# Queries of five pairs transposed from the landed fp32, masks drawn in slot order, and a new order of work

## The chip, the cores and the metric

The kernel runs on one core of a Trainium2 chip. The metric is the device time of one execution in microseconds; lower is better. The engines are named as the profile names them: PE is TensorE's matmul stream and PEld its weight loads, DVE is VectorE, ACT is ScalarE, POOL is GpSimd, SP is the engine that issues nearly all transfers. Each engine takes its instructions in the order in which they were recorded.

## The reference

Attention over 4 batches, 8 heads, 768 positions and a head size of 64, followed by a gated feed-forward block on the 3072 tokens of 512 features.

```python
causal = rel >= 0
is_sink = pos[None, :] < int(n_sink)                 # n_sink = 4
in_win = (rel >= 0) & (rel < int(window))            # window = 64
stream_keep = causal & (is_sink | in_win)
# heads 0, 2, 6 use causal; the other five use stream_keep
a = softmax(where(mask, scale * q @ k.T, -1e9)) ; x = a @ v
g = x @ w_gate                                       # 512 x 1536
out = (g * sigmoid(g) * (x @ w_val)) @ w_out         # 1536 x 512
```

Inputs and output are fp32; inside, the kernel multiplies in fp16 and accumulates in fp32.

## The kernel before, in words

**Tiles.** A pair is 256 positions of one batch; there are 12, and `QP` lists them, the pairs of the first two batches interleaved. A pair has two tiles of 128 positions, so there are 24 tiles. The 24 tiles go in six groups of four to the feed-forward part. Positions are held in slot order: a pair's load puts position 2p + j at partition p, and after the transposes the even positions of a tile come first, then the odd ones.

**A pair's way in.** `load` brings q, k and v of a pair (512 KB each) into a buffer of the ring `raw` (14 buffers). `cast` turns k and q into fp16 in a buffer of the ring `hq`. For pairs 0 to 4 (`XQK = XK = 5`) TensorE then transposes: `transposes(n, w)` does eight 128x128 blocks for q (w = 0, line 438) or k (w = 1, line 435) into PSUM, and `evacq` and `evack` copy them to `qT` and `kT`. From pair 5 on the transfers transpose instead (`dmaq`, `dmak`), from the buffers `hqz` and `hq`. `hqz` is cleared once by `fill3`.

**A tile.** `scores` (line 547) multiplies keys and queries into PSUM, `exps` (line 557, ACT) takes the exponential, `values` (line 577) multiplies by v, `recip` and `norm` divide, `xtranspose` turns the result for the feed-forward part. A tile's scores come in two to four units; units of tiles 0 and 1 are up to 512 elements wide and may sit in the ring `gv`, those of later tiles up to 1024 wide and always sit in the one buffer of the ring `sc`, which is two PSUM banks.

**Masks.** GpSimd draws four 128x128 patterns (`OWN`, `DIAG`, `FAR`, `BAND0`) into `nat` in natural order, 0 where a key is kept and -32768 where not. For tiles 0 to 3 the scores get them added on TensorE: a matmul of `nat` by the permutation matrix `perm` into the same PSUM bank (`marks`). For later tiles the exponentials are multiplied by 0/1 masks `m0`, `m1`, `m2` (line 565). `mask_order` (line 245) multiplies `perm` and `nat` once into PSUM, and `mask_fill` (line 255, DVE) writes the 0/1 masks from there in nine operations.

**Feed-forward.** `gate` (line 778) multiplies a group's tiles by one 128-column block of the gate or the value weights; `tanh` (784, ACT), `stt1` (788, DVE) and `stt2` (795, DVE) form h; `outproj` (813) multiplies by the output weights, `oevac` copies out of PSUM, `store` writes. The weights are cast by `wcast` from fp32 loads of 512 KB.

**What sets the order.** All work is recorded as tasks (`P.add`), each with the engines that may run it. The strings `ORDER` and `WAYS`, worked out beforehand, give the sequence in which the tasks are recorded and the engine each one takes; nothing is rescheduled afterwards. A number of 3700 + n in `ORDER` stands for n more `warm` matmuls (line 292), fillers of 512 columns whose result nobody reads. Waits follow from what a task reads and from the ring buffer that it takes. The task names used below are: `cq`/`ck`/`cx` n.x, casts of q, k, v of pair n; `trn.0` and `trn.1`, transposes of q and k; `evqn.sx` and `evkn.x`, their evacuations; `sct.u`, `ext.u`, scores and exponentials of unit u of tile t; `valt.o`, `nmt.o`, values and norm; `xtrt`, the transpose of tile t; `gateg.j.c`, gate of group g, block j; `wc g1`, the cast of the second gate weight load; `mkdiag`, `mkfar`, the mask drawing; `mfill`, the mask fills.

Read out of `ORDER` and `WAYS`, the order before is, up to the first gate:

```
PE   warm(10) tr0.0 warm(2) tr0.1 warm(6) sc1.3 tr1.0 sc1.2 sc1.0 sc0.1 sc0.0 tr1.1 val0.0 val0.1
     sc1.1 sc2.0 val1.0 tr2.0 val1.1 sc3.0 warm(1) val2.1 xtr0 sc3.1 val3.1 xtr1 warm(1) val2.0
     tr2.1 gate0.2.0
ACT  cq0.0 cq0.1 evq0.00 evq0.10 evq0.11 evk0.0 ex1.3 ex1.2 ex1.0 evq1.00 ex0.1 ex0.0 ex1.1 ex2.0
     nm0.0 ex3.0 cx1.1.0 xe1 ex3.1
DVE  fill ck0.0 evq0.01 evk0.1 fill3 cx0.1.0 evq1.01 cx0.1.1 ck1.0 evq1.10 evq1.11 evk1.1 evk1.0
POOL mkdiag ck0.1 mkfar cq1.0 cq1.1 cx0.0.0 ck1.1 fill1 cx0.0.1 cq2 cx1.0.0 cx1.0.1 ck2
SP   q0 k0 q1 v0 k1 q2 v1 k2 g1 g0 wv1 q3 wv0 k3 g2
```

On SP `g` and `wv` are loads of gate and value weights. Behind the first gate, `xtr2` and `sc4.0` follow within the next seven tasks of PE.

Of the kernel before, what the change touches and what calls it, by code (L numbers as in the profile page):

```python
# [7 lines left out]
FP = mybir.dt.float32  # L8
FH = mybir.dt.float16
AF = mybir.ActivationFunctionType  # L10
ALU = mybir.AluOpType
# [5 lines left out]
    "080400091L1O021M1N01xh1T1U1W1V1Xxi1Y1a1Z1K0B0A1Rxm1t1u25261P0C280E031Q2D1r2G1S1s271n1d1o1b2E2j2I"  # L17
    "2F1e2H1i1c1f2K1p0D1q292A2J2L1g0F1y2p2k1h1j2M2C2r2q1v0j1w1k151x2V2Wxh2N1z202O2P0i0p1l2B1m2X2Z2a23"
    "242b2Yxh2Q2s9Z2R2S2c2t2T2d210H2U9j11309k312e9l109F0o2h2u9G162i9o9a9H9c2v0I0k0G9b9d3Q059e062x9f9p"
    "9q9m3W2y369n3D3Y9K0q9g22072z129I3E3X9J2f9N9L9M3A3B3M3R3Z3a9O189h2l2m9t9u9i2w3e9v9y0K329P333f9z9r"  # L20
    "9s34A00n350t3b2n37199w9x2o3C0m3cA13F3G1H3H3IA249134FAN3J4G9QAO9R3h9S9T3i3K1IAQ3g3pAP1E3z0s401FAS"
    "4HAR3d9UAV0J3S3TATAUAW3N9V3t380l3L3VAI0L9W3u1BAL3vAJ393j3k3l3mAKA8AM4A410N3n9X3o0r0O9Y3q4I423wA9"
    "3xA34o0M3U434J44ADAA4N3r4p3y3sAG453OAEAF0Q2g1CA44O4K4WABAH4q463P4L4BA54748A64Z4aBQ4MACA70xBTBR4c"
    "4l4dAwAx4vBS4CBU4xBf4PBg4DAyBh4Q4RBVBWAzBXB0ArAsB14bAtBiBj4S4w4TB24y5253B3B44U4VBGBH4z50B5BJBL5V"
    "0RBI4f0w5WBY4X4E4hBK5X1AB64gB75D4e5G5H0v17BZ1D510yB80u14BkAX5J4iB9BA0zBl4Y4j1J5K5fAY0PBM1GBNBm55"
    "4m564r54BaBEAZAa4k5L5d4s594t4u575A5cAu585B5E5eBb5g5hAvAc0T5CAdBc0bAe5I5Q5MBO0SBP5Z0UBB5N5O5RAfBC"
    "BDAhBd5P0VAi5S5TAjAb5oBFAk5pBnBeAg625Y634n64Bo5FAmAn5iAo5UCJ6761ApCd7SCKCL5r5s5tCeCf6BCgCh6ACsBp"
    "Bq5q5a68COCtCu5j7T5k695yAq656F5bCv5u7Q0X6i5v6GCPCQAlBr0W6g6CBs0a6O6p5w5x6DCwC95lCACB6ECMBuCR6UCS"
    "BvCNBwCn6V6I6hCoCpCb0Z6J6oBx6qBt0Y5zCY6kCZCaCcCT6X665m6Y6nBzCi6K6R6S7P0e6HC0C1Cl6LCjCkCmCCCUCV6M"
    "6d7W6uCD0g6T5n6v6NCE6P6w7XC260CHCxCFCGCI6rC46s7N6mC5Cy6z706Z6aCW6jCXCz6W6b6xCqC36QD08a6y7x6c6fCr"  # L30
    "6eC6C7By7O7VD2757U6tD37RD1787971D5D47AEF72E0E1E20c73D67B7C0hD7EDD876EGC87j7kEHEIEJEAEBECD9DA7D7g"
    "7t8i7l0d7vDRDB82DgDC7hEE7i7E7477DhDiE37m7n7z7FE5DSDTE6DDDEDF837GE47wE8Db7H6l7uE7E98eDUDVDcEK7I7Y"
    "7JENELEM7qEO7Z7aDHDIDd7KDe7LDq80817o0fDrDs7p877rDfDJ7yDKDWDXDYDt7b7cDu88DlDm847sDo8GDnDp857d8ZDv"
    "Dw8A7e8BDx89Dy8Y7MDM8JDG8KDjDzDk8LDN8MDZ7fEoEp8NFDFEDa868V8CFG8D8P8Q8c8E8gEqEjFFDOFH8dDPEkFIElDL"
    "EmFJ8f8h8pFL8FFKFMF88H8REP8qF9FA8jEn8k8bEQ8SEyEzFBERFC8m8lESETFS8xF0Et8nF18OEu8T8U9394F2EvEUEV8I"
    "ErEw8W8t8X90FTFUFcEW8oEx918r8uFdFe92FfEXDQ8sFX8v8wFg8y98EZFYEYEaFZ9996EsF3F495F58zEbEc979AF6FN9B"
    "9C9DEeEfF7FOFPFaFbFVEgFW9EGGEhGJEiGHGIGKGkGlGuGvGnGwGmFhFQGoGxGyFRG6G7FiFjFkFlEdG8GVGWGYGXGaG9Gb"
    "GcGZFmGpFnGqGrG1G2GAG3GsGBGtGCGdGeGDFoGLGMFpG4G5GQFrGRGSFsGTFtGOFuGNGfGgFvGPFqFwGhGEGFFxFyFzG0GU"
    "GiGzGjH0H1H4H2H3H5H6H7H8H9HAHBHEHFHCHDHGHHHJHIHKHL"
)  # L40
WAYS = (
    "000000000000000000000000000000000000000000000000000000000000002020222122002102002000012221100010"
    "001000000000100000000000000000101221222020011101100000000000000000000110022100001101001000000000"
    "100000100000000000002222220000100000100000000010000100100000000002022220110100000100000020000000"
    "100000010012202210000001001000000000100000010000000002221202000000000000000001000010022211210000"
    "000000000000220000001000000110202022000000000000000000000000000000000000012122000000000000000000"
    "010000210002221100000000010000001200010010000002001120011000000000000000000210000000000000000000"
    "000000000000000000000000000000000000000000000000000000000000000000000000000000000000000000000001"
    "000000000000000000000000000000000000000000000000000000000000000000000100001000000000000000000000"
    "000000000000000000000000000000000000000000000000000000000000000100000000000000000000000000000000"  # L50
    "000000000000000000000000000000000000010000100001000000000000000000000000000000000000000000000000"
    "000000000000000000000100000000000000000000000000000000000000000000000000000000000000000000000000"
    "10000000001000000010"
# [52 lines left out]
def kernel(  # L106
# [97 lines left out]
    perm = const.tile([128, 128], FH, name="perm")  # L204
# [7 lines left out]
    OWN, DIAG, FAR, BAND0 = range(4)  # L212
# [4 lines left out]

    def keep(n, base, qstep, kstep):
        nc.gpsimd.affine_select(
            out=nat[:, n], in_=nat[:, n], compare_op=ALU.is_ge, fill=OFF, base=base,  # L220
            pattern=[[qstep, 2], [2 * qstep, 64]], channel_multiplier=kstep)

    def make_diag():
        nc.gpsimd.memset(perm, 0.0)
        nc.gpsimd.affine_select(
            out=perm, in_=perm, compare_op=ALU.not_equal, fill=1.0, base=0,
            pattern=[[-1, 2], [-2, 64]], channel_multiplier=1)
        nc.gpsimd.memset(nat, 0.0)
        keep(DIAG, 0, 1, -1)
        keep(BAND0, WIN - 1, -1, 1)  # L230
        nc.gpsimd.memset(nat[0:NSINK, BAND0], 0.0)
        keep(BAND0, 0, 1, -1)

    def make_far():
        keep(OWN, WIN - 1, -1, 1)
        keep(OWN, 0, 1, -1)
        keep(FAR, WIN - 1 - 128, -1, 1)
        nc.gpsimd.memset(nat[0:64, FAR], OFF)
        nc.gpsimd.memset(nat[0:NSINK, FAR], 0.0)

    mask_ps = []

    def mask_order():
        ps = buf("o", [128, 4, 128], FP, "mk")
        nc.tensor.matmul(ps.rearrange("p n q -> p (n q)"), perm,
                         nat.rearrange("p n q -> p (n q)"), start=True, stop=True)
        mask_ps.append(ps)

    def mask_fill(x):
        ps = mask_ps[0]  # L250
        for dst, src in ((m2[:, 0:1], OWN), (m2[:, 1:4], DIAG), (m2[:, 4:5], FAR),
                         (m1[:, 0:2], OWN), (m1[:, 2:4], FAR),
                         (m0[:, 0:4], BAND0), (m0[:, 4:6], DIAG), (m0[:, 6:7], BAND0),
                         (m0[:, 7:8], DIAG))[5 * x:5 + 5 * x]:
            nc.vector.tensor_scalar(
                out=dst, in0=ps[:, src].unsqueeze(1).to_broadcast([128, dst.shape[1], 128]),
                scalar1=-1.0 / OFF, op0=ALU.mult, scalar2=1.0, op1=ALU.add)

# [32 lines left out]

    T_masks = [P.add("mkdiag", ["POOL"], make_diag)]
# [5 lines left out]
    T_mord = P.add("mord", ["PE"], mask_order, deps=T_masks, takes=["o"], after=[T_warm])  # L301
    T_fill = [P.add(f"mfill{x}", ["DVE"], (lambda x=x: mask_fill(x)), deps=[T_mord])
              for x in range(2)]
    P.uses(T_mord, "o", *T_fill)
# [72 lines left out]
    def cast(n, kd, x):  # L377

        r = landed[kd, n].rearrange("p (h j d) -> p h j d", j=2, d=64)
        if n >= XQK and kd == "q":  # L380
            recast(T_c[n, kd, x],
                 hqz[:, :, x, :, x * 64:(x + 1) * 64].rearrange(
                     "p j (r k) d -> p k r j d", r=2),
                 r.rearrange("p (k s r) j d -> p s k r j d", r=2, s=2)[:, x])
            return
        if n not in hqs:
            h = buf("hq", [128, 2, 1024], FH, "hq")
            hqs[n] = [h[:, 0].rearrange("p (j r x) -> p j r x", j=2, r=2),
                      h[:, 1].rearrange("p (k a x) -> p k a x", k=2, a=4)]
        if kd == "k":  # L390
            ks = slice(0, 2) if x is None else slice(x, x + 1)
            recast(T_c[n, kd, x],
                 hqs[n][1][:, ks].rearrange("p k a (s d) -> p k s a d", s=2),
                 r.rearrange("p (k s r) j d -> p k s (r j) d", r=2, s=2)[:, ks])
            return
        js = slice(0, 2) if x is None else slice(x, x + 1)
        recast(T_c[n, kd, x],
             hqs[n][0].rearrange("p j r (k d) -> p k r j d", d=64)[:, :, :, js],
             r[:, :, js].rearrange("p (k r) j d -> p k r j d", r=2))
# [28 lines left out]
    def transposes(n, w):  # L428
# [504 lines left out]
```

The softmax here doesn't subtract the row's maximum and nothing guards it: scores larger than these inputs give would overflow.

## Time and profile before

| | |
|---|---|
| median of 3 runs | 257.31 us (257.26 to 257.41) |
| the profiled execution | 257.29 us, span 255.5 us |
| first score matmul | 9.23 us |
| first gate matmul | 21.38 us |
| last matmul group ends near | 251.7 us |
| transfers in all | 42.53 MB |

The span is what the profiler recorded of the program; the execution's own time has 1.8 us around it. Times within a trace count from the start of the span. A timeline row gives the start, the duration, the engine, the source line, the operation, what it writes and reads, and in brackets how long the engine sat idle before it and what released it. A group row gives the number of instructions, the busy time and the mean duration of one. Durations of matmuls include a latency that overlaps with the next one, so a run of matmuls is counted by its start and end and not by the sum of its rows.

### The profile page before, as it was taken

Reading aid. Unit: us, or ns where it says so; the run is one execution under the profiler, and the core shown is the slowest. Engines: PE = TensorE matmul, PEld = TensorE weight load, DVE = VectorE, ACT = ScalarE, POOL = GpSimd, SP = SyncE. Lnnn points to the kernel's source line nnn. Section 1 sums busy time; section 2 is a strip of 40 time slices with the busy share of each in tenths; the row PEclk is TensorE's granted clock in tenths of the full one; section 3 lists DMA queues with packets and bytes.
Section 4 is the critical chain, followed back from the end, with each engine's and each line's share of the span. In section 5 each row is a group of like instructions: output and inputs, shape, how many; then the busy total and the mean of one; then the engine's idle time right before and its main releaser. Section 6 shows DMA issues by size and latency. Waiting matters only on the chain.

```text
span 255.5 us, 4847 instructions
## 1 busy us (share of the span) xinstructions
PE 246.7 (97%) x1812; PEld 136.7 (54%) x1812; DVE 177.1 (69%) x360; ACT 135.3 (53%) x214; POOL 81.5 (32%) x118
## 2 busy tenths in 40 slices
PE   7889899999999999999999999999999999999994
PEld 3567765665555554545555555555555554444442
DVE  3777899997897566859976587778557766463511
ACT  3767998766488445645555663637753412322100
POOL 4674888695674412410450230342000100000000
PEclk9999999999999999999999999999999999999999
DMA  7999999996999958998959947254022211300444
GB/s 188 290 310 326 318 337 316 304 212 136 388 181 223 295 140 158 266 167 189 224 114 204 239 91 165 44 116 92 0 62 64 62 23 41 82 0 0 100 96 99
DMA packets 80536, 42.53 MB, mean 166 GB/s; under 512 B 32768, under 2 KB 76032, under 8 KB 80512
## 3 DMA queue, kind: packets, MB, share of 16 engines
q1 hardware_dynamic: 80352, 42.09, 68.8%
q8 instruction: 14, 0.23, 0.4%
q10 hardware_dynamic: 160, 0.13, 0.2%
q14 instruction: 10, 0.08, 0.1%
HBM read 28.31 MB, written 6.29 MB: 135 GB/s over the span
## 4 chain that ended last, share of the span: by engine, by line
PE 84%; DVE 6%; DMA 3%; ACT 3%; SPq 2%; issue 1%; POOL 1%; DVEq 0%; POOLq 0%; ACTq 0%
PE gv L778 44%; PE o_ps L813 24%; PE sc L547 9%; PE av L577 5%; DMA raw<-in_k_dram 3%; ACT e L557 2%; SPq L317 2%; DVE h L795 1%; DVE sil L788 1%; DVE xb L594 1%; DVE vt L181 1%; DVE e L565 1%; ACT qT L175 1%; DVE qT L177 1%; PE xtr L610 1%
## 5 line engine op out<-in xcount | busy, mean ns | idle before, releaser
L557 ACT ACTIVATE e<-sc 128x1024 f16<-128x1024 f32 (+3 forms) x71 | 62.2, 878 | 32.1 <-PE sc L547 31.3
L778 PE MATMUL gv<-xt,wv_sb 128*128 128x512 f16 (+1 forms) x304 | 73.5, 368 | 0.4 <-DVE sil L788 0.3
L778 PE MATMUL gv<-xt,wg_sb 128*128 128x512 f16 (+1 forms) x304 | 73.0, 368 | 0.0
L784 ACT ACTIVATE sig<-gv 128x512 f32<-128x512 f32 (+1 forms) x76 | 43.0, 574 | 51.1 <-PE gv L778 49.4
L813 PE MATMUL o_ps<-wo_sb,h 128*128 128x512 f16 (+2 forms) x300 | 69.5, 370 | 0.0
L788 DVE SCALAR_TENSOR_TENSOR sil<-sig,gv 128x512 f32<-128x512 f32 (+1 forms) x76 | 49.3, 654 | 25.1 <-ACT sig L784 24.0
L795 DVE SCALAR_TENSOR_TENSOR h<-sil,gv 128x512 f16<-128x512 f32 (+1 forms) x76 | 49.3, 654 | 20.3 <-PE gv L778 18.9
L813 PEld LDWEIGHTS <-h 128*128 128x128 f16 x300 | 28.5, 98 | 30.0
L778 PEld LDWEIGHTS <-wg_sb 128*128 128x128 f16 x304 | 28.8, 98 | 27.2 <-issue 0.2
L778 PEld LDWEIGHTS <-wv_sb 128*128 128x128 f16 x304 | 28.7, 98 | 25.9 <-issue 0.6
L547 PE MATMUL sc<-qT,kT 128*128 128x256 f16 (+1 forms) x276 | 37.4, 257 | 0.5 <-ACT e L557 0.5
L565 POOL TENSOR_TENSOR e<-e,m 128x640 f16<-128x640 f16 (+1 forms) x16 | 26.3, 1641 | 33.9 <-ACT e L557 32.2
L547 PEld LDWEIGHTS <-kT 128*128 128x128 f16 x276 | 24.6, 98 | 12.3 <-issue 1.3
L577 PEld LDWEIGHTS <-e 128*128 128x128 f16 x472 | 19.6, 97 | 11.1 <-DVE xb L594 2.2
L577 PE MATMUL av<-vt,e 128*128 128x65 f16 x472 | 22.0, 193 | 1.3 <-DVE xb L594 0.5
L175 ACT COPY o_sb<-o_ps 128x512 f32<-128x512 f32 (+1 forms) x14 | 8.1, 578 | 26.0 <-PE o_ps L813 26.0
L594 DVE TENSOR_TENSOR xb<-av,rc 128x256 f16<-128x256 f32 x47 | 19.9, 424 | 1.6
L177 POOL CAST vt<-raw 64x512 f16<-64x512 f32 x24 | 15.5, 644 | 16.0 <-DMA raw<-in_v_dram 14.9
L177 POOL CAST hq<-raw 128x1024 f16<-128x1024 f32 (+1 forms) x15 | 14.2, 947 | 15.7 <-DMA raw<-in_k_dram 14.4
L177 POOL COPY vt<-vt 2x330 f16<-2x330 f16 x14 | 6.3, 453 | 37.6 <-PE av L577 37.3
L582 DVE RECIPROCAL rc<-av 128x4 f32<-128x4 f32 x48 | 8.5, 177 | 10.4 <-PE av L577 10.1
L565 DVE TENSOR_TENSOR e<-e,m 128x1024 f16<-128x1024 f16 (+1 forms) x22 | 14.7, 668 | 0.8 <-ACT e L557 0.8
(58 smaller groups left out, 130.9 us busy)
## 6 DMA issues: line engine op xcount, KB each, us to landing
raw<-in_q_dram SPq DMA_DIRECT2D x12, 512.0 KB, 6.5
raw<-in_k_dram SPq DMA_DIRECT2D x12, 512.0 KB, 7.0
raw<-in_v_dram SPq DMA_DIRECT2D x12, 512.0 KB, 7.0
out_dram<-o_sb SPq DMA_DIRECT2D x46, 128.0 KB, 2.4
raw<-in_moe_w_gate_dram SPq DMA_DIRECT2D x6, 512.0 KB, 7.8
raw<-in_moe_w_val_dram SPq DMA_DIRECT2D x6, 512.0 KB, 7.9
raw<-in_moe_w_out_dram SPq DMA_DIRECT2D x6, 512.0 KB, 6.7
xt<-xb SPq DMA_TRANSPOSE x16, 2.4
```

The costliest lines, as they stand in the source:

```text
L175: nc.scalar.copy(out=dst, in_=src)
L177: ENG[task.way].tensor_copy(out=dst, in_=src)
L547: nc.tensor.matmul(sc[c // 4][:, c % 4:c % 4 + n, :], weights, moving, start=first, stop=last)
L557: nc.scalar.activation(out=e[:, 0:n], in_=whole_sc.pop((t, u))[:, 0:n], func=AF.Exp, scale=scale)
L565: ENG[task().way].tensor_tensor(out=ev, in0=ev, in1=mm, op=ALU.mult)
L577: nc.tensor.matmul(av[:, n, 0:65], ee, vv, start=(m == 0), stop=(m == len(bl) - 1))
L594: nc.vector.tensor_tensor(out=xbs[t][:, :, odd, :], in0=av[:, :, 0:64], in1=rc.to_broadcast([128, 4, 64]), op=ALU.mult)
L778: nc.tensor.matmul(ps, wsb[:, kk, j * 128:(j + 1) * 128], xt[:, kk, c[0]:c[1]], start=(kk == 0), stop=(kk == 3))
L784: nc.scalar.activation(out=sg[g, j, c], in_=gs[g, j, c], func=AF.Tanh, scale=0.5)
L788: nc.vector.scalar_tensor_tensor(out=sl[g, j, c], in0=sg.pop((g, j, c)), scalar=1.0, op0=ALU.add, in1=gs.pop((g, j, c)), op1=ALU.mult)
L795: nc.vector.scalar_tensor_tensor(out=hs[g, j][:, c[0]:c[1]], in0=sl.pop((g, j, c)), scalar=0.5, op0=ALU.mult, in1=vs.pop((g, j, c)), op1=A ...
L813: nc.tensor.matmul(o_open[g, tt, x], hs[g, j][:, tt * 128:(tt + 1) * 128], wo_sb[:, j, lo:hi], start=(j == 0), stop=(j == NJ - 1))
```

## The change

Four things are changed together.

**Queries of pairs 0 to 4** are no longer cast. TensorE transposes them from the landed fp32 buffer with an fp32 identity, in two tasks of four blocks, one for each half s, each into a PSUM bank of its own (`ring_q`: the ring `tr` for s = 0; `gv` for s = 1 of pairs 0 and 1, `o` for later ones). Four evacuations for each pair, 64x512, fp32 to fp16. Before, pairs 0 and 1 had four of 64x512 and pairs 2 to 4 two of 64x1024, all from fp16. The `hq` buffer halves.

**Masks** are drawn by GpSimd in slot order, each pattern in two halves of 64 partitions, so scores add them through `ident` and `perm` is gone; `identf`, the fp32 identity, is drawn in its place. `mask_order` is gone. `mask_fill` reads `nat` from SBUF instead of PSUM and may run on ACT or DVE.

**The order** is a new one. `fill3` goes from DVE to POOL, `mfill0` and `mfill1` stay on DVE and come early. Read out of the new strings, up to the first gate:

```
PE   warm(10) tr0.0.0 tr0.0.1 warm(8) tr0.1 warm(5) tr1.1 sc1.3 sc1.1 sc1.2 sc0.0 tr1.0.0 warm(3)
     val0.1 tr1.0.1 sc1.0 tr2.0.1 sc0.1 sc2.0 val1.1 tr2.1 sc3.1 val0.0 val1.0 tr2.0.0 val2.1 sc3.0
     xtr0 val2.0 xtr1 sc4.0 xtr2 val3.1 gate0.2.0
ACT  ck0.0 ck1.0 evk0.1 evk0.0 ex1.3 cx0.0.0 ex1.1 evk1.1 ex0.0 evq1.01 evq1.00 ex1.2 ex1.0 ex2.0
     ex0.1 ex3.1 evq2.00 evq2.01 ex3.0 sk1.1 xe1 ex4.0
DVE  fill evq0.00 evq0.01 mfill0 evq0.10 ck1.1 evq0.11 evk1.0 mfill1 evq1.11 evq1.10
POOL mkident mkdiag mkfar fill3 ck0.1 cx0.1.0 fill1 cx0.1.1 cx0.0.1 cx1.0.0 cx1.0.1 wc_v1 cx1.1.1
     sk0.1 wc_g1
SP   q0 k0 k1 v0 q1 q2 k2 v1 wv1 g1 g0 v2 q3 wv0 k3
```

For pairs 3 and 4 the evacuations of q were two on ACT (pair 3) and two on DVE (pair 4); they are now three on ACT and one on DVE (pair 3) and one on ACT and three on DVE (pair 4).

The diff, cut to its core (the two strings are left out):

```diff
-    perm = const.tile([128, 128], FH, name="perm")
+    identf = const.tile([128, 128], FP, name="identf")
...
-    OWN, DIAG, FAR, BAND0 = range(4)
+    DIAG, BAND0, OWN, FAR = range(4)
...
+    def odds(j):
+        return slice(64 * j, 64 * j + 64)
+
     def keep(n, base, qstep, kstep):
+        for j in range(2):
+            part = nat[odds(j), n]
+            nc.gpsimd.affine_select(
+                out=part, in_=part, compare_op=ALU.is_ge, fill=OFF, base=base + kstep * j,
+                pattern=[[0, n.stop - n.start], [qstep, 2], [2 * qstep, 64]],
+                channel_multiplier=2 * kstep)
+
+    def first_keys(n, count, value):
+        for j in range(2):
+            nc.gpsimd.memset(nat[64 * j:64 * j + count // 2, n], value)
+
+    def make_identf():
+        nc.gpsimd.memset(identf, 0.0)
         nc.gpsimd.affine_select(
-            out=nat[:, n], in_=nat[:, n], compare_op=ALU.is_ge, fill=OFF, base=base,
-            pattern=[[qstep, 2], [2 * qstep, 64]], channel_multiplier=kstep)
+            out=identf, in_=identf, compare_op=ALU.not_equal, fill=1.0,
+            base=0, pattern=[[-1, 128]], channel_multiplier=1)
 
     def make_diag():
-        nc.gpsimd.memset(perm, 0.0)
-        nc.gpsimd.affine_select(
-            out=perm, in_=perm, compare_op=ALU.not_equal, fill=1.0, base=0,
-            pattern=[[-1, 2], [-2, 64]], channel_multiplier=1)
-        nc.gpsimd.memset(nat, 0.0)
-        keep(DIAG, 0, 1, -1)
-        keep(BAND0, WIN - 1, -1, 1)
-        nc.gpsimd.memset(nat[0:NSINK, BAND0], 0.0)
-        keep(BAND0, 0, 1, -1)
+        nc.gpsimd.memset(nat[:, DIAG:OWN + 1], 0.0)
+        keep(slice(BAND0, OWN + 1), WIN - 1, -1, 1)
+        first_keys(BAND0, NSINK, 0.0)
+        keep(slice(DIAG, OWN + 1), 0, 1, -1)
 
     def make_far():
...
+        nc.gpsimd.memset(nat[:, FAR], 0.0)
+        keep(slice(FAR, FAR + 1), WIN - 1 - 128, -1, 1)
+        first_keys(FAR, 64, OFF)
+        first_keys(FAR, NSINK, 0.0)
...
-    def mask_order():
-        ps = buf("o", [128, 4, 128], FP, "mk")
-        nc.tensor.matmul(ps.rearrange("p n q -> p (n q)"), perm,
-                         nat.rearrange("p n q -> p (n q)"), start=True, stop=True)
...
+    def mask_fill(task, dst, src):
+        src = nat[:, src].unsqueeze(1).to_broadcast([128, dst.shape[1], 128])
+        if task.way == "ACT":
+            nc.scalar.activation(out=dst, in_=src, func=AF.Identity, scale=-1.0 / OFF, bias=1.0)
+        else:
+            nc.vector.tensor_scalar(out=dst, in0=src, scalar1=-1.0 / OFF, op0=ALU.mult,
+                                    scalar2=1.0, op1=ALU.add)
...
+    FILLS = [[(m0[:, 0:4], BAND0), (m0[:, 4:6], DIAG), (m0[:, 6:7], BAND0), (m0[:, 7:8], DIAG),
+              (m2[:, 1:4], DIAG), (m2[:, 0:1], OWN), (m1[:, 0:2], OWN)],
+             [(m2[:, 4:5], FAR), (m1[:, 2:4], FAR)]]
...
+    def ring_q(n, s):
+        return "tr" if s == 0 else "gv" if n < 2 else "o"
+
+    def transposes_q(n, s):
+
+        raw = landed["q", n].rearrange("p (h x) -> p h x", h=H)
+        tr = trs[n, s] = buf(ring_q(n, s), [128, 4, 128], FP, "trq")
+        for p in range(4):
+            nc.tensor.transpose(tr[:, p], raw[:, PAIRS[p][s]], identf)
+
+    def evacq(n, s, j):
+        copy(T_ev[n, s][j], qT[n % 2][s * 64:s * 64 + 64, s, :, j, :],
+             trs[n, s][j * 64:j * 64 + 64])
...
-        terms = [(c, n, perm, nat[:, m].unsqueeze(1).to_broadcast([128, n, 128]))
+        terms = [(c, n, ident, nat[:, m].unsqueeze(1).to_broadcast([128, n, 128]))
...
+                tr = P.add(f"tr{n}.0.{s_}", ["PE"], (lambda n=n, s_=s_: transposes_q(n, s_)),
+                           deps=[T_load["q", n], T_identf], takes=[ring], after=[T_warm])
```

## The prediction, before the result was known

> **What bounds the kernel now.** I read the page's busy shares and its chain first, then busy time by stretch, then the timeline up to the first gate, then the prices of the rows that the change touches.
>
> ```profile
> PE 246.7 (97%) x1812; PEld 136.7 (54%) x1812; DVE 177.1 (69%) x360; ACT 135.3 (53%) x214; POOL 81.5 (32%) x118
> ...
> PE 84%; DVE 6%; DMA 3%; ACT 3%; SPq 2%; issue 1%; POOL 1%; DVEq 0%; POOLq 0%; ACTq 0%
> ```
> ```profile
> 0.00:9.20 9.20, 7.75 (x35) 3.52 (x36) 3.94 (x8) 4.11 (x7) 4.91 (x20) 1.00 0.86 219
> ...
> 22.10:30.00 7.90, 7.27 (x77) 6.00 (x74) 7.10 (x24) 6.45 (x12) 5.58 (x11) 1.00 1.16 315
> 30.00:50.00 20.00, 19.21 (x187) 12.47 (x187) 18.57 (x45) 17.71 (x27) 15.64 (x13) 1.00 1.13 321
> 50.00:240.00 190.00, 189.83 (x1316) 100.59 (x1315) 135.34 (x258) 95.99 (x152) 47.53 (x63) 1.00 0.62 138
> 240.00:255.50 15.50, 11.72 (x67) 5.84 (x64) 2.41 (x5) 1.65 (x3) 0.00 (x0) 1.00 0.36 87
> ```
> The columns after the stretch are its length and the busy time of PE, PEld, DVE, ACT and POOL. From 50 us on TensorE is full (189.83 of 190), so whatever delay it has by then reaches the end whole. Before that there are three parts: a head to 9.2 us, in which PE runs mostly fillers (19 of 21 `warm` matmuls); the attention lead-in to the first gate; and a stretch from 22 to 50 us in which DVE and ACT are nearly full and PE loses 0.63 + 0.79 us. The change acts on all three.
>
> ```profile
> 6.74 0.69 DVE L181 TENSOR_REDUCE hq<-raw 128x512 f16<-128x512 f32 x1 [3.46 <-DMA raw<-in_k_dram]
> 6.77 0.61 POOL L177 CAST hq<-raw 128x512 f16<-128x512 f32 x1 [3.22 <-DMA raw<-in_k_dram]
> ...
> 7.48 0.62 PE L435 MATMUL tr<-ident,hq 128*128 128x128 f16 x8
> ...
> 9.23 0.22 PE L547 MATMUL sc<-nat,perm 128*128 128x128 f16 x1
> ...
> 21.38 0.60 PE L778 MATMUL gv<-xt,wg_sb 128*128 128x256 f16 x4
> ...
> 21.94 0.62 ACT L175 CAST wg_sb<-raw 128x512 f16<-128x512 f32 x1 [0.19 <-DMA raw<-in_moe_w_gate_dram]
> ```
> DVE and POOL were both idle when k0 landed, so its two halves were cast at once, transposed at 7.48, and the first score stood at 9.23. The first gate came at 21.38; the tenth load landed at 21.94.
>
> **What the Trainium skill says.** "TensorE: Matmul & The Clock Gate", Terms: matmuls have a transpose mode, 4 times faster for fp32, so one pass and not four; its section on weight-path modes adds that fast weight load is off for fp32 and its section on LDWEIGHTS prices 128 columns at 128/1.2 = 107 ns. No fp32 transpose is in this trace. "VectorE: DVE Perf Modes", perf-mode tier table: fp32 out of PSUM runs at one element per cycle, 16-bit out of PSUM at up to two. The trace agrees, 418 ns against 687 ns for 512 elements (below). "Advanced Engine Details and Errata", VectorE Performance Modes: VectorE's second SBUF port is shared with GpSimd, and GpSimd instructions and two-port Vector instructions block each other. The trace agrees:
>
> ```profile
> 29.96 0.48 DVE L565 TENSOR_TENSOR e<-e,m 128x640 f16<-128x640 f16 x1
> ...
> 30.12 1.21 POOL L177 CAST wg_sb<-raw 128x1024 f16<-128x1024 f32 x1 [0.48 <-DMA raw<-in_moe_w_gate_dram]
> ...
> 38.14 1.04 POOL L177 CAST wv_sb<-raw 128x1024 f16<-128x1024 f32 x1 [0.67 <-DMA raw<-in_moe_w_val_dram]
> ...
> 38.38 1.14 DVE L565 TENSOR_TENSOR e<-e,m 128x640 f16<-128x640 f16 x1
> ```
> The same 640-element multiply takes 0.48 us ahead of a POOL cast (which then takes 1.21 instead of 1.04) and 1.14 us when it starts inside one, ending after it.
>
> **The change part by part.** Prices:
>
> ```profile
> L177 DVE COPY o_sb<-o_ps 128x512 f32<-128x512 f32 x10 | 6.9, 687 | 6.6 <-PE o_ps L813 6.6
> ...
> L177 DVE COPY qT<-tr 64x512 f16<-64x512 f16 x4 | 1.6, 418 | 0.2 <-ACT qT L175 0.2
> ...
> L219 POOL TENSOR_SCALAR_AFFINE_SELECT nat<-nat 128x128 f16<-128x128 f16 x6 | 1.7, 297 | 0.2
> ```
> *Fp32 transposes.* Eight fp16 ones take 0.62 us, 0.078 each. One fp32 costs between that and 107 + 53 = 160 ns if nothing overlaps (estimate from the page above), or four times 160 if it runs four passes. I take 0.125: eight in 1.0 us, four in 0.5. Forty of them; the 24 of pairs 0 to 2 lie in the lead-in, the 16 of pairs 3 and 4 on a full PE: +0.8 us there (0 to 1.3; 9 at four passes).
>
> *Query casts.* Gone: two on ACT and two on POOL for pairs 0 and 1, one POOL cast of about 1.04 us each for pairs 2 to 4. The evacuations become fp32: 687 ns on DVE where 418 stood (no 64x512 fp32 row exists; the o_sb row has the same length), 586 on ACT as before.
>
> *POOL's head.* identf takes the place of perm (0.206 + 0.295, ready at 1.83). mkdiag: one memset of 384 elements, about 0.42 (memsets of 128 and 512 take 206 and 525 ns, 0.83 ns an element), four affine selects of 256, 256, 384, 384 (297 ns at 128; 0.30 each if length cost nothing, 0.59 and 0.89 if it cost everything; I take 0.45 and 0.6), two small memsets at 0.26 start to start. mkfar: memset 0.28, two selects 0.62, four small memsets 1.04. That ends near 6.8 us. Then fill3 comes over from DVE (0.912 there): 2048 fp16 elements on POOL at 0.83 ns are 1.8 us. So ck0.1, which could run at 6.77 before, starts near 8.6 (7.8 to 9.2) and ends at 9.25. tr0.1 follows at once: done near 9.8, against 8.1 before.
>
> *DVE's head.* The ten opening warm matmuls end at 5.6 as before; q0 has landed by then (its cast began at 4.93). tr0.0.0 ends at 6.1. evq0.00 and evq0.01: 6.3 to 7.7. Then mfill0, moved up from about 26 us, stands ahead of evq0.10, ck1.1 and evq0.11. Its seven operations, 1792 elements, now from SBUF, cost 0.9 us at the skill's four elements a cycle, 2.9 at the PSUM rows' prices; I take 1.2. They use the shared port while POOL is in its long memset, so they end between 8.9 and 10.4. Three more at 0.69 follow: 11.0 to 12.5. The first score needs evq0.11: it starts at T = 11.1 to 12.7, and I take 11.6, against 9.23. The five warm matmuls and k1's transposes before it fit into that wait.
>
> *Loads and edits without a price.* SP issues the same 123 transfers; k1 moves from fifth to third, q1 from third to fifth. The third lands near 8.5 (between k0 at 6.74 and v0 at 10.37, estimate), the fifth near 12.2 (k1's cast began at 12.16). So k1's casts are done before T, and q1, which needs no cast now, saves the 0.6 us that k1's cast took there; that gain is in the walk below, where q1's transposes find PE already later than 12.2. Marks multiplied by ident for perm and the halved hq buffer cost nothing: same shapes, and no take of hq waited.
>
> *From T to the first gate.* ACT sets the pace through the single two-bank `sc` buffer. Ahead of sc4.0 it has six exps of 512 (0.545 start to start, from 1.09 for two at 10.78), three of 1024 (1.02), one value cast (0.62) and five copies (0.53): 9.6 us. Twice it waits for a score to be rewritten, 1.1 us before ex2.0 and 0.55 before ex3.1. With 0.4 for the first score, ex3.0 ends at T + 11.7; sc4.0 (0.44), xtr2 and val3.1 (0.2 each) put the gate at T + 12.5 = 24.1. In the new load order its gate weights are the tenth load: landed 21.9, cast on POOL 1.04, so never before 23.05. The order before had less ahead of the gate: sc4.0 and xtr2, 0.7 us, stand behind it. Equal progress is thus 21.38 + 0.7 = 22.1, and the lag is 2.0 us (1.5 to 3.1).
>
> *From the gate to 50 us.* DVE loses the mask fills (1.61 + 1.41 us at 25.99 and 28.63) and gains 1.4 us of fp32 evacuations (pair 4: two of 0.69 become three of 0.69, pair 3: none becomes one); POOL loses two casts, 2.1 us; PE loses the mask-order matmul, 0.2. These are the engines that are full there. Of the 1.6 us that PE loses after 22.1 (0.63 + 0.79 + 0.17) between nothing and all goes; I take half, -0.8.
>
> Sum: 2.0 + 0.8 - 0.8 - 0.2 = +1.8 us. Against the profiled execution (span 255.5, time 257.29, 1.8 around it) that is 259.1; the median of the three runs, 257.31, is the same within 0.02. The parts' bounds give 257.8 to 260.8 for this case.
>
> **Rivals.** *The relief outweighs the head.* Mechanism: the 4 to 5 us of DVE and POOL work removed before 50 us let PE run without stalls there. If mask fills do not collide with POOL and the fp32 evacuations cost less, T is 10; the gate then waits for its weights at 23.05, a lag of 0.95; with all 1.6 us of stalls gone, no fp32 surcharge and the 0.2: -0.85, so 256.4. It decides once T is under 10.9 or so (lag under 1.4 and less than 0.3 us surcharge). For it: DVE 18.57 of 20 and ACT 17.71 of 20 in that stretch. Against: DVE's own four evacuations, mask fills and ck1.1 alone reach 11.0.
> *They cancel*: the lag of 1.5 is paid back by the stalls, 257.3.
> *Four-pass transposes*: 0.64 each on 40 of them, +9 us on pairs 3 and 4 and some 4 in the lead-in: 270. Against it speaks only the skill's sentence.
>
> **How the numbers follow.** Less than 0.2% (0.5 us) can't be told from no change. Forecast case 0.56, relief 0.26, cancel 0.13, four passes 0.05. The forecast is 259.1. The range takes in the relief case, and a lag of 3.1 with a full surcharge: 256.0 to 261.3, leaving out the four passes and the far ends. Faster 0.26, same 0.14, slower 0.60.
>
> **What would show it.** Right: ck0.1 on POOL starting after 8 us with its data long landed, the first score after 11 us, DVE evacuations of q near 0.69, the first gate near 24 us, and PE full from then with few stalls. Wrong: fp32 transposes of over 0.2 us each; a first score before 10.5; mask fills of 0.15 us that never stretch; or PE losing as much as before between the gate and 50 us, which puts the time over 260.

## The result, and the profile after

The changed kernel takes 263.49 us (263.00 to 264.37, 4 runs), the kernel before 257.35 us beside it: a ratio of 1.0243, 95% interval 1.021 to 1.0276. It is slower, as forecast, but by 6.1 us and not by 1.8. The profiled execution took 263.0 us with a span of 261.2; against the profiled execution before (257.29) that is 5.7 us, and this sum is taken apart below. One execution of one kernel further down (`b_double`, 265.55 us) ran in a slower state of the chip, at a lower granted clock, and is left out of its figures.

The page after: its busy line, its chain by engine, and the new group of fp32 evacuations.

```profile
PE 249.8 (96%) x1816; PEld 140.6 (54%) x1816; DVE 171.7 (66%) x344; ACT 142.1 (54%) x228; POOL 89.7 (34%) x120
...
PE 78%; DVE 13%; ACT 3%; DMA 2%; issue 2%; SPq 1%; ACTq 0%; POOL 0%; POOLq 0%; DVEq 0%
...
L177 DVE CAST qT<-trq 64x512 f16<-64x512 f32 x12 | 8.2, 686 | 6.7 <-PE trq L442 6.5
```

DVE is less busy than before in sum (171.7 us for 177.1), yet its share of the chain has doubled, from 6% to 13%. The work went down and the waiting for it went up. Busy time by stretch shows where. The columns are the length, the busy time of PE, PEld, DVE, ACT and POOL, the granted clock, the DMA share and GB/s. First the kernel before from its first score to its first gate, then the changed kernel, its first row likewise:

```profile
9.23:21.38 12.15, 10.12 (x132) 7.78 (x131) 9.00 (x25) 8.82 (x17) 7.65 (x13) 1.00 1.16 311
```
```profile
11.94:27.24 15.30, 11.57 (x135) 9.13 (x133) 10.71 (x26) 10.68 (x19) 6.84 (x12) 1.00 1.14 311
...
9.20:22.10 12.90, 10.09 (x106) 7.54 (x106) 9.44 (x23) 8.41 (x15) 5.50 (x12) 1.00 1.16 311
22.10:30.00 7.90, 6.29 (x77) 5.36 (x78) 6.34 (x18) 6.01 (x13) 2.86 (x4) 1.00 1.11 306
30.00:50.00 20.00, 19.19 (x194) 14.60 (x192) 17.42 (x44) 15.76 (x30) 17.10 (x16) 1.00 1.11 332
50.00:240.00 190.00, 189.14 (x1325) 100.69 (x1324) 128.87 (x247) 105.87 (x163) 56.65 (x66) 1.00 0.60 137
```

From the first score to the first gate PE idles 3.73 us, where it idled 2.03 before. From 30 us on it is nearly as full as before (19.19 us for 19.21, then 189.14 for 189.83). DVE and ACT are equally busy on the way to the gate (10.71 and 10.68 us of 15.30), so busy time alone does not say which of them sets its pace. The head and the first gate in the timeline of after:

```profile
6.91 1.81 POOL L411 MEMSET hqz<- 128x2048 f16 x1
...
8.02 2.09 DVE L256 TENSOR_SCALAR m<-nat 128x512 f16<-128x512 f16 x7
...
8.78 0.68 POOL L177 CAST hq<-raw 128x512 f16<-128x512 f32 x1
...
11.94 0.22 PE L547 MATMUL sc<-nat,ident 128*128 128x128 f16 x1
...
27.24 0.60 PE L777 MATMUL gv<-xt,wg_sb 128*128 128x256 f16 x4
```

POOL's third fill, its late cast and the mask fills on DVE stand where the prediction put them, and the first score comes at 11.94 us (forecast 11.6). The first gate comes at 27.24 us, where 24.1 was forecast. What PE waited for longest between 5 and 60 us (total, times, longest, in us):

```profile
PE trq L442 <- DVE kT L177: 1.1, 1, 1.1
PE xtr L610 <- DVE xt L177: 1.1, 1, 1.1
PE tr L431 <- DVE hq L181: 1.0, 2, 0.6
```

All three releasers are on DVE. Its timeline there:

```profile
16.08 1.39 DVE L177 CAST qT<-trq 64x512 f16<-64x512 f32 x2 [3.11 <-PE trq L442]
...
18.07 1.21 DVE L181 TENSOR_REDUCE hq<-raw 128x1024 f16<-128x1024 f32 x1
19.30 0.68 DVE L177 CAST qT<-trq 64x512 f16<-64x512 f32 x1
...
20.67 0.69 DVE L177 CAST qT<-trq 64x512 f16<-64x512 f32 x1
21.40 0.69 DVE L177 COPY kT<-tr 128x1024 f16<-128x1024 f16 x1
...
22.28 0.68 DVE L181 TENSOR_REDUCE vt<-raw 64x512 f16<-64x512 f32 x1
...
24.21 0.99 DVE L181 TENSOR_REDUCE vt<-vt 2x330 f16<-2x330 f16 x2
25.24 0.42 DVE L177 COPY xt<-xtr 128x512 f16<-128x512 f16 x1
```

After 16.08 no row has a bracket, neither those shown nor the reciprocals and norms between them: DVE is never seen to wait until 26 us. The chain of work that ended last, followed back from the end, says that the others wait for it: from 16.08 to 25.68 us every piece of it is DVE's, but for issue times of at most 0.31 us between them (start, us, what; some of its pieces):

```profile
15.58 0.48 PE trq L442 x4
...
16.08 0.69 DVE qT L177
...
18.07 1.21 DVE hq L181
...
21.40 0.69 DVE kT L177
...
25.24 0.44 DVE xt L177
...
25.72 0.40 PE xtr L610 x4
```

The copy of k2 out of the bank `tr` (21.40) stands behind two query evacuations of 0.68 us and a cast of k2, and PE can write the next transpose into that bank only after it. The new order gives DVE three pieces ahead of the first gate that it did not have there before: `ck2` (18.07, on POOL before), `cx1.1.0` (22.28, on ACT before) and `sv0.1` (24.21, on POOL and behind the gate before). `xe0` at 25.24 waits behind the last.

### The profile page after: what moved, and what is told of

Read it like the earlier page. It is cut to its first block, busy times and chain, and to the rows that moved or that the text cites. A ratio compares the mean times of both kernels' runs of the same rounds, so it can differ in the third digit from the quotient of the medians.

```text
span 261.2 us, 4842 instructions
## 1 busy us (share of the span) xinstructions
PE 249.8 (96%) x1816; PEld 140.6 (54%) x1816; DVE 171.7 (66%) x344; ACT 142.1 (54%) x228; POOL 89.7 (34%) x120
## 4 chain that ended last, share of the span: by engine, by line
PE 78%; DVE 13%; ACT 3%; DMA 2%; issue 2%; SPq 1%; ACTq 0%; POOL 0%; POOLq 0%; DVEq 0%
PE gv L777 41%; PE o_ps L812 22%; PE sc L547 7%; PE av L577 4%; DVE qT L177 3%; DMA raw<-in_v_dram 2%; DVE vt L181 2%; DVE sil L787 2%; PE warm L298 2%; DVE xb L594 1%; DVE h L794 1%; ACT e L557 1%; DVE m L256 1%; DVE hq L181 1%; PE trq L442 1%
## 5 line engine op out<-in xcount | busy, mean ns | idle before, releaser
L557 ACT ACTIVATE e<-sc 128x1024 f16<-128x1024 f32 (+4 forms) x71 | 62.2, 879 | 33.6 <-PE sc L547 32.7
L777 PE MATMUL gv<-xt,wv_sb 128*128 128x512 f16 (+1 forms) x304 | 72.1, 368 | 0.2
L777 PE MATMUL gv<-xt,wg_sb 128*128 128x512 f16 (+1 forms) x304 | 71.7, 368 | 0.3 <-DVE sil L787 0.3
L565 POOL TENSOR_TENSOR e<-e,m 128x1024 f16<-128x1024 f16 (+1 forms) x20 | 35.9, 1798 | 25.9 <-ACT e L557 21.8
L577 PEld LDWEIGHTS <-e 128*128 128x128 f16 x472 | 20.3, 97 | 9.3 <-DVE xb L594 1.0
L175 ACT COPY o_sb<-o_ps 128x512 f32<-128x512 f32 (+2 forms) x19 | 10.7, 562 | 23.6 <-PE o_ps L812 23.6
L177 POOL COPY kT<-kT 128x8 f16<-128x8 f16 (+1 forms) x12 | 2.0, 186 | 48.2 <-PE sc L547 48.2
L565 DVE TENSOR_TENSOR e<-e,m 128x1024 f16<-128x1024 f16 (+1 forms) x18 | 13.1, 730 | 1.4 <-ACT e L557 1.4
L177 DVE CAST qT<-trq 64x512 f16<-64x512 f32 x12 | 8.2, 686 | 6.7 <-PE trq L442 6.5
```

The lines of the kernel that those rows point to most:

```text
L175: nc.scalar.copy(out=dst, in_=src)
L177: ENG[task.way].tensor_copy(out=dst, in_=src)
L557: nc.scalar.activation(out=e[:, 0:n], in_=whole_sc.pop((t, u))[:, 0:n], func=AF.Exp, scale=scale)
L565: ENG[task().way].tensor_tensor(out=ev, in0=ev, in1=mm, op=ALU.mult)
L577: nc.tensor.matmul(av[:, n, 0:65], ee, vv, start=(m == 0), stop=(m == len(bl) - 1))
L777: nc.tensor.matmul(ps, wsb[:, kk, j * 128:(j + 1) * 128], xt[:, kk, c[0]:c[1]], start=(kk == 0), stop=(kk == 3))
```

## The experiments

Fourteen kernels, each compared with the kernel before on the same chip. "First score" and "first gate" are the starts of these matmuls in the trace, in us.

| run | time us | ratio to before (95%) | first score | first gate |
|---|---|---|---|---|
| changed kernel | 263.49 | 1.0243 (1.021 to 1.0276) | 11.94 | 27.24 |
| b_mask | 257.35 | 0.9994 (0.9981 to 1.0006) | 9.53 | 21.70 |
| b_query | 265.07 | 1.0299 (1.0276 to 1.0323) | 9.50 | 24.82 |
| b_both | 262.31 | 1.0184 (1.0157 to 1.0211) | 9.32 | 24.60 |
| b_act | 260.37 | 1.0117 (1.01 to 1.0134) | 9.54 | 23.08 |
| b_double | 259.3 | 1.0071 (1.0043 to 1.0099) | 9.27 | 22.69 |
| a_mfill | 263.97 | 1.0261 (1.024 to 1.0281) | 11.31 | 26.35 |
| a_ways | 264.46 | 1.0277 (1.0262 to 1.0293) | 11.98 | 28.66 |
| a_head | 263.22 | 1.0224 (1.0197 to 1.0252) | 10.17 | 26.87 |
| a_both | 264.54 | 1.0285 (1.0269 to 1.03) | 10.25 | 29.39 |
| a_act | 262.30 | 1.0195 (1.0162 to 1.0229) | 11.96 | 26.27 |
| a_act4 | 262.66 | 1.02 (1.0174 to 1.0225) | 11.98 | 26.87 |
| a_all | 261.81 | 1.0173 (1.0137 to 1.0208) | 10.55 | 25.52 |
| a_all2 | 260.92 | 1.0132 (1.011 to 1.0155) | 10.17 | 24.21 |
| a_twice | 263.49 | 1.0229 (1.0206 to 1.0252) | 11.94 | 27.24 |

### One part at a time, in the order of before

The first theory was that the new order alone overloads VectorE's queue and that the parts cost little; its rival was that the queries' part costs wherever it stands. The edits of the order are given by task names, as in the description of the kernel. `b_query` has the queries' part alone, `b_mask` the masks' part alone, `b_both` both, each in the order of before.

```diff
 # b_query and b_both, in the order of before
-cq0 .. cq4
-trN.0             evqN.s0           (N = 2, 3, 4)
+trN.0.0 trN.0.1   evqN.s0 evqN.s1   on the engine that evqN.s0 had
-warm behind the first transposes that use ring "o"
```

> Masks alone: the kernel before with its own order, masks drawn in slot order on GpSimd and the 0/1 masks filled from SBUF at their old place; the mask-order matmul is gone. Theory 1: 256.8 to 257.6, the drawing ends before k0 lands and the fills are shorter than from PSUM. Theory 2: over 258, since the longer drawing and the shared port hold the casts of k0 and the fills.

> Queries alone: the kernel before with its own order, in which each query transpose becomes the two fp32 ones in the same place, the query casts are left out and the evacuations keep their engines; masks as before. Theory 1 (the new order put too much on VectorE's queue ahead of the first gate; the parts alone cost little): 257.5 to 259, the first gate within 1.5 us of 21.4. Theory 2 (fp32 transposes and fp32 evacuations are the cost wherever they stand): 260 to 263, gate after 24. Two late filler matmuls are dropped, since their PSUM bank is now used.

> Both parts in the order of before (query transposes in place, masks in place, no new plan). Theory 1: 257 to 259, so that 4.5 us or more of the 6.1 belong to the new order. Theory 2: 262 to 264, as the changed kernel.

The masks' part costs nothing: 257.35 us. The queries' part costs 5 us with the masks' part beside it, in the old order. The first theory fell as it was stated: with both parts in it the old order takes 262.31 us, not 257 to 259. It is, if anything, better than the new one (263.49, the intervals just touching). (`b_query` alone is slower still. It keeps `mask_order`, whose bank in ring `o` is held until the mask fills have read it, and the fp32 transposes of pair 3 wait 2.6 us for it; that wait is of this run's own making.)

What PE waits for up to 30 us in `b_both` is new. The wait:

```profile
PE av L577 <- DVE rc L582: 2.6, 1, 2.6
```

and what DVE does meanwhile in `b_both`, below the same evacuations in the kernel before, where PE waited 0.39 us at this place:

```profile
16.21 1.39 DVE L177 COPY qT<-tr 64x1024 f16<-64x1024 f16 x2 [1.16 <-PE tr L438]
```
```profile
17.37 2.80 DVE L177 CAST qT<-trq 64x512 f16<-64x512 f32 x4 [1.36 <-PE trq L442]
20.20 0.18 DVE L582 RECIPROCAL rc<-av 128x4 f32<-128x4 f32 x1
```

Where before two evacuations of pair 2's queries took 1.39 us, there are now four taking 2.80. The reciprocal for which PE's next `av` product waits stands behind them in DVE's queue. "VectorE: DVE Perf Modes" of the Trainium skill, perf-mode tier table, lets 16-bit data out of PSUM run at up to two elements a cycle and fp32 at one; the trace agrees, with 64x1024 fp16 in 0.69 us before and 64x512 fp32 in 0.69 us now. (Pairs 0 and 1 had four pieces of 64x512 already, 0.42 us each in fp16; there the time grows by two thirds.) So the second theory: the doubled evacuation time on DVE's in-order queue, with single PSUM banks behind it, makes PE wait, in either order.

### The doubled evacuation by itself, and taken away

`b_double` is the kernel before, fp16 transposes and all, with pair 2's evacuations issued twice. `b_act` is `b_both` with two of the four evacuations moved to ScalarE.

```diff
 # b_double
+        for again in range(2 if n == 2 else 1):
             copy(T_ev[n, s][x], qT[n % 2][c, s, ps].rearrange("c p j n -> c j p n"),
                  trs[n, 0][c, :, ps])
 # b_act
-evq2.10 evq2.11   DVE
+evq2.10 evq2.11   ACT
```

> The kernel before, unchanged but for one thing: each of the two fp16 copies by which VectorE evacuates pair 2's queries is issued twice, so that they take 2.79 us in place of 1.39 us, as the fp32 ones do. No fp32 transpose, no bank shared in a new way, no order changed. Theory 1', the doubled evacuation time on VectorE's in-order queue is the cost: PE waits about 1.5 us more on the row reciprocals that stand behind it, the first gate product comes 1.3 to 2.0 us later than 21.4 us, and the time is 258.7 to 260.3 us; if the gap also costs clock, 0.7 to 0.9 in the slice of 20 to 25 us. Rival 2, the fp32 transposes and their banks: no change, 257.2 to 257.6.

> Both parts of the change in the order of before, with the two fp32 evacuations of pair 2's queries of head 1 moved from VectorE to ScalarE. Theory 1': the wait of 2.6 us of PE on the row reciprocals that stood behind them goes, the granted clock stays at 1.00 in the slices of 20 to 30 us, time 258.5 to 259.5 us instead of 262.3. Rival: ScalarE is as late as VectorE was and the exponentials come behind the evacuations; the wait turns up as PE on ACT e, time 261.5 to 263.

Doubling alone costs 1.8 us (0.71% of 257.3; 1.1 to 2.5 by the interval), without any fp32 transpose. Its PE row after the evacuations:

```profile
19.79 0.28 PE L578 MATMUL av<-vt,e 128*128 128x65 f16 x4 [1.83 <-DVE rc L583]
```

The gate is 1.3 us later than before. The clock stayed at 1.00 in its trace. `b_act` removes 1.9 us from `b_both`, and the wait of PE on `rc` falls from 2.6 to 0.7 us, but the time stays above the 258.5 to 259.5 that was expected: 3 us over the kernel before remain. Not all of the 1.9 us is the wait itself. In the trace of `b_both` the granted clock falls to half behind that wait (last section); its three executions with a mean clock of 0.991 to 0.993 took 262.27 to 262.62 us, the fourth, at 0.999, took 260.94. By that one execution some 1.4 us of what `b_act` wins is the fall of the clock that followed the wait. The waits that `b_act` has left are short and spread over several names, the longest 0.7 us each (PE on exponentials, `sil`, `rc`), and 1.17 us of evacuation now stand on ScalarE. Its first gate is 1.7 us later than before (23.08 for 21.38). A share of it may also be TensorE's own: forty fp32 transposes at 0.108 us (measured below) instead of 0.078 are 1.2 us if nothing hides them, an estimate. How the 3 us divide is not settled.

### The same load in the changed kernel

Four first tries did not help.

```diff
 # a_mfill   DVE: -mfill0, -mfill1 early     +both just ahead of mask4.0
 # a_ways    ck2, cx1.1.0, sv0.1:            -DVE  +POOL
 # a_head    POOL: -fill3 ahead of ck0.1     +just ahead of fill1
 #           DVE:  -mfill0 ahead of evq0.10  +just ahead of mfill1
 # a_both    a_ways and a_head together
```

> The changed kernel with one move: both mask fills stand on VectorE just ahead of the first mask multiply, not ahead of evq0.10. Theory 1: the first score comes about 2 us earlier (9.9 instead of 11.9) and 1 to 2 us of it reach the end: 261.3 to 262.5. Theory 2: no change, 263 to 264.

> The changed kernel with three pieces of its lead-in moved from VectorE to the idle GpSimd, nothing else: the cast of k2 (1.21 us), the copy cx of head 1 (about 0.9 us) and the first save of v (0.99 us). Theory 1', VectorE's in-order queue sets the first gate: some 2.9 us leave that queue between 16 and 25.7 us, so the first gate product comes at 24.3 to 25.3 us instead of 27.2 and the time is 260.5 to 261.5 us. Rival 2, the fp32 transposes and the shared PSUM bank hold TensorE themselves: the gate moves by 0.5 us at most, time 263.0 to 263.7.

> The changed kernel with GpSimd's third fill placed behind its cast and its first copy, and VectorE's first mask fill placed just ahead of the second one. If the head (the first score at 11.94 us instead of 9.23) passes through to the end, the first score comes at 10.3 to 10.6 us and the time falls by 1.2 to 1.5 us, to 262.0 to 262.3. If VectorE's queue between 16 and 26 us sets the gate whatever the head does, first score the same 10.3 to 10.6 but gate at 26.7 to 27.2 and time 263.0 to 263.5.

> The edits of the two runs before together. Theory 1': they act on different stretches of one chain and add, gate at 23.0 to 24.0 us and time 259.0 to 260.2. If one covers the other, no better than the better of the two by more than 0.3 us.

`a_mfill` brings the gate 0.9 us forward, but its fills (1.35 us, at 27.11) then hold the first `stt1`, and PE waits 0.9 us for that. `a_head` brings the first score 1.8 us forward and the gate only 0.4. The displaced fill adds a wait of its own (PE on `vt` from POOL, 1.0 us), and DVE is more loaded than in the changed kernel: its nine mask fills, 1.35 us in `a_mfill` where no POOL fill is near and 2.09 + 0.34 us in the changed kernel, take 4.21 us at 10.71, beside that fill and POOL's casts of v. The granted clock falls in its trace too, from 26 us on; its two executions at a mean clock of 0.993 took 263.70 and 263.74 us, those at 0.998 and 1.000 took 262.74 and 262.16. `a_ways` took load off DVE and put it into another queue that was not free. POOL's rows in `a_ways`:

```profile
19.13 1.04 POOL L177 CAST wv_sb<-raw 128x1024 f16<-128x1024 f32 x1 [0.31 <-DMA raw<-in_moe_w_val_dram]
20.11 1.04 POOL L177 CAST hq<-raw 128x1024 f16<-128x1024 f32 x1
```

The cast of k2 ran at 18.07 on DVE; on POOL it stands behind a weight cast that waits for its transfer, and starts at 20.11. PE waited 2.4 us for it. In `a_both` the value cast and the fill behind each other cost more still (PE on `vt` from POOL, 3.1 us). Both traces also show the clock at half for some microseconds. These two runs put a new wait in the place of the one removed, so they don't decide between the theories; they show that POOL's idle time could not be used in that place.

The next four put the work mainly where the trace of after has ScalarE idle at the moment when the data are ready.

```diff
 # a_act    evq2.10, evq2.11:  -DVE  +ACT, both ahead of ex2.0
 # a_act4   a_act, and         cx1.1.0 -DVE +ACT ahead of evq2.00;  sv0.1 -DVE +ACT
 # a_all    a_act4, and        fill3 behind cx0.0.1;  mfill0 just ahead of mfill1
 # a_all2   a_all, but         sv0.1 -ACT +POOL
```

> The changed kernel with pair 2's two evacuations of head 1 moved from VectorE to ScalarE, into the 1.12 us for which ScalarE idles from 17.4 us. If VectorE's queue sets the first gate: 1.37 us leave it ahead of the evacuation of k2, the gate comes at 25.8 to 26.2 us instead of 27.2 and the time is 262.0 to 262.5. If ScalarE's pace sets it, as the prediction had it: the 1.17 us are added to ScalarE, gate at 27.2 to 28.3 and time 263.5 to 264.6.

> As the run before, and the copy cx of head 1 and the first save of v moved from VectorE to ScalarE too, each into a gap of ScalarE: 3.0 us off VectorE between 16 and 25.7 us. VectorE's queue theory: gate at 24.2 to 25.2 us, time 260.4 to 261.5 us. ScalarE's pace: no better than the changed kernel's 263.5.

> As the run before, with GpSimd's third fill placed behind the first four copies cx and VectorE's first mask fill just ahead of the second, so that the head is as short as that of the kernel before: first score at 10.0 to 10.5 us. With VectorE's queue relieved the earlier first score should now come through to the end: gate at 22.8 to 24.0 us, time 259.0 to 260.3 us. If it is lost again, as it was with VectorE loaded: 260.4 to 261.5.

> The run a_all with the first save of v on GpSimd instead of ScalarE, where it took 0.94 us ahead of the copy xe1 and let PE wait 1.1 us for it (the single xtr bank). If it was only this placing that kept VectorE's relief from arriving, the wait PE xtr on ACT xt goes, the gate comes at 24.2 to 24.8 us instead of 25.5 and the time is 260.4 to 261.0. If something else sets the gate in the new order: 261.5 to 262.1, as a_all.

`a_act` takes 1.37 us off DVE and the gate comes 1.0 us earlier, the time falls by 1.2 to 262.3 (its interval overlaps that of the changed kernel a little). The prediction's view, that ScalarE sets the pace, would have put it at 263.5 to 264.6. `a_act4` missed, 262.66 us, and so did `a_all`, 261.81; both show the same wait. First ScalarE, then PE in `a_all`:

```profile
23.28 0.94 ACT L175 COPY vt<-vt 2x330 f16<-2x330 f16 x2
24.23 0.29 ACT L175 COPY kT<-kT 128x8 f16<-128x8 f16 x2
24.43 0.57 ACT L175 COPY xt<-xtr 128x512 f16<-128x512 f16 x1
```
```profile
25.05 0.38 PE L610 MATMUL xtr<-ident,xb 128*128 128x128 f16 x4 [1.08 <-ACT xt L175]
```

The save of v stands ahead of `xe1`, the copy that empties the single `xtr` bank, and PE waits 1.08 us for it. With that save on POOL (`a_all2`) the wait goes, the gate comes at 24.21 and the time is 260.92 us, both as expected: 2.6 us under the changed kernel, the intervals well apart (those of `a_all` and `a_all2` overlap). Here the shorter head, lost in `a_head`, does come through: between `a_act4` and `a_all` the first score and the gate both move by 1.4 us. The fill stands three places further back than in `a_head` (behind `fill1` and two more copies of v), so the load on DVE, the wait on POOL and the fall of the clock may all have hidden it there.

### The transposes behind the gate

`a_twice` issues the sixteen fp32 transposes of pairs 3 and 4 twice.

```diff
-        for p in range(4):
+        for p in [0, 1, 2, 3] * (2 if n > 2 else 1):
             nc.tensor.transpose(tr[:, p], raw[:, PAIRS[p][s]], identf)
```

> The changed kernel with the sixteen fp32 transposes of pairs 3 and 4 issued twice, nothing else. They stand between 31 and 42 us, where PE is busy over nine tenths of the time. If TensorE's time is the bound there, as the prediction's terms for the transposes and the mask product assume, all sixteen show in the end: 16 times 0.108 us is 1.7 us, time 265.0 to 265.4; if gaps take them up, 263.5 to 264.2.

The median does not move, 263.49 us. The first group of four in the changed kernel, then of eight in `a_twice`:

```profile
31.29 0.61 PE L442 MATMUL trq<-identf,raw 128*128 128x128 f32 x4
```
```profile
31.30 1.04 PE L442 MATMUL trq<-identf,raw 128*128 128x128 f32 x8
```

Each group takes 0.43 to 0.44 us more, 0.108 us for one transpose, and the end of the span is 0.5 us later. Over 1 us of the 1.7 did not reach the end; 0.7 us of that shows as less idle time of PE behind the gate (0.97 us for 1.67), the rest was not located. PE's time behind the gate is thus not paid in full, and the +0.5 us that sixteen transposes cost by their prices is more likely too much than too little.

No version with fp32 queries came under the kernel before; the best, `b_act`, is 3.0 us over it.

## Why the prediction was wrong in size

| step | predicted | measured |
|---|---|---|
| fp32 transpose, each | 0.125 us | 0.108 us |
| first score, T | 11.6 us | 11.94 us |
| from T to the first gate | 12.5 us | 15.30 us |
| lag at the gate (against 22.1) | 2.0 us | 5.14 us |
| from the gate to PE's end (+0.8 - 0.8 - 0.2) | -0.2 us | +0.42 us |
| behind PE's end | 0 | +0.15 us |
| sum | +1.8 us | +5.7 us |

The measured lag is 27.24 - 22.1. Of the 3.9 us by which the sum missed, 2.8 lie between the first score and the first gate. PE ends at 257.29 and 251.73 us, so behind the gate 5.56 - 5.14 = 0.42 is added.

*The transposes and POOL's head* came out as forecast. One pass, not four: the rival of 270 us is out. The third fill took 1.81 us, the cast of k0's second half started at 8.78 (8.6), the mask fills ended at 10.1 (8.9 to 10.4).

*The step that failed is "From T to the first gate": "ACT sets the pace".* The sum was made along ScalarE's list, 12.5 us, and DVE's list was not added up. ScalarE's own work was priced well: 9.5 us from its first exponential at 12.68 to the end of `ex3.0` at 25.06, forecast 9.6. Its waits in between came to 2.90 us (1.12, 0.73 and 1.05), not 1.65, and two of the three lead back to DVE: PE's transposes of k2 waited for `ck2`, and its next transposes of pair 2's queries for the copy of k2 (1.11 us). From the end of `ex3.0` to the gate it took 2.18 us, not 0.84, because `xtr1` waited 1.07 us for `xe0` on DVE. The first exponential began 0.3 us later behind the first score than reckoned, and with that the 2.8 us are complete. The DVE list printed with the change breaks off at `evq1.10`, the row at 16.08 where the full stretch begins, although more stands ahead of the gate: `ck2`, `evq2.10` and `evq2.11` at 0.69 each, the copy of k2, `cx1.1.0`, `sv0.1` and `xe0` among the reciprocals and norms, without a wait from 16.08 to 26 us (9.70 us busy of 10.12). The list of before lacks its last entries in the same way, two evacuations of pair 2's queries and `xe0` among them. The runs show the same from both sides: relief of DVE brings the gate forward (`a_act` by 1.0 us, and `a_all2` together with the head by 3.0), and the doubled evacuation by itself delays the kernel before (`b_double`, by 1.3 us at the gate). The prediction did price the fp32 evacuation at 0.69 us, and did count 1.4 us of it for pairs 3 and 4, where DVE loses the mask fills; it did not count it for pair 2, where it lies on the path.

*The relief of -0.8 us was not there.* Stalls of PE behind the gate were 1.59 us before (1.42 and 0.17) and are 1.67 (0.81 to 50 us and 0.86 after). They sank where DVE was relieved and came back later. PE's busy time rose by 0.35 us (228.03 to 228.38), about the transposes (0.48 us by their prices) less the mask product (0.2); the surcharge of 0.8 was nearer 0.5 by the measured price.

*What made the prediction wrong by its own test* came true in part: between the gate and 50 us PE lost less than before (0.81 us for 1.42, in a shorter stretch), but with what came after 50 us it lost as much, and the time is over 260. The larger part of that is the late gate and not these stalls. Of the rivals, the relief case is out: T did not fall under 10.9 and no stall was saved on balance.

*Open:* how the 3.0 us that `b_act` keeps over the kernel before divide between TensorE's longer transposes, the evacuations now on ScalarE and the queues behind them; and whether an order planned anew for DVE's load could come under 260.4 us, which was not tried; and how much of `b_both` is the order or the parts and how much the clock, since only one of its executions escaped the fall (260.94 us).

## What to carry to other kernels

Dropping a cast ahead of a transpose can move its price to the evacuation: here the evacuation of a pair's queries from PSUM took four pieces of 0.69 us in fp32 where fp16 took two, and where single banks waited behind that queue, TensorE paid. Ahead of the first product of a long full stretch, write out and add up the list of every in-order engine, with the point from which it has no gap left, and not only the list of the one that looks busiest; and when a piece is moved to an idle engine, ask what that engine's queue is waiting for at that moment. An early delay that seems worth nothing when removed may only be hidden by another one beside it.

## What was not expected of the hardware

In these traces the granted clock fell at gaps that were shorter than thought. Busy time by single microseconds in `b_both`, behind the gap of 2.62 us that ends at 20.99:

```profile
21.00:22.00 1.00, 1.00 (x16) 0.89 (x16) 0.97 (x4) 0.00 (x0) 0.00 (x0) 1.00 1.16 321
22.00:23.00 1.00, 1.00 (x15) 0.79 (x12) 0.46 (x2) 0.00 (x0) 0.61 (x1) 0.51 1.19 298
...
24.00:25.00 1.00, 1.00 (x10) 0.90 (x9) 0.70 (x3) 0.97 (x2) 0.67 (x1) 0.50 1.13 328
25.00:26.00 1.00, 1.00 (x17) 0.85 (x15) 0.64 (x3) 0.31 (x1) 0.00 (x0) 0.78 1.20 295
```

The granted clock (the third number from the end) is halved from 22 to about 25.4 us, a full microsecond after PE has resumed. In `a_head` no single wait of PE is over 1.1 us, but it is busy for only 2.56 of the 5 us from 20 to 25, and behind that stretch, from 26 us on, the clock is 0.50 too:

```profile
24.00:25.00 1.00, 0.02 (x1) 0.02 (x1) 0.97 (x3) 0.51 (x3) 0.26 (x1) 1.00 1.17 288
...
27.00:28.00 1.00, 1.00 (x8) 0.67 (x6) 0.87 (x3) 0.05 (x1) 0.00 (x0) 0.50 1.19 295
```

"TensorE: Matmul & The Clock Gate" of the Trainium skill, Part 1 on the clock gate, says that the clock halves after at least one idle window of some 3.4 us, and that the window runs freely. Half speed and a stay of about 3.4 us agree (in `a_both`, behind a gap of 3.1 us, it stays twice as long); that a wholly idle window of that length is needed does not, since a gap of 2.6 us and a half-filled stretch were enough here. The gap of 1.83 us in `b_double`, and `a_all` with PE busy 2.67 of the same 5 us, did not trigger it. Nor did `a_act4`, with PE busy 1.92 of the 4 us from 23 to 27, which is less than in `a_head`: the busy share of a stretch alone does not decide, and what does stays open. Each of these falls puts some microseconds of TensorE at half speed, so part of what `b_query`, `b_both`, `a_ways`, `a_head` and `a_both` lost is clock. For two of them the executions without a fall give a size, 1.4 us in `b_both` (one execution against three) and 1.0 to 1.6 us in `a_head` (two against two); in the other three every execution has a mean clock of 0.994 or less, and it was not separated.
